# First q of an attention and soft-MoE kernel: loaded in f32 on SyncE's queue and cast by ScalarE

## The chip, the cores and the metric

The kernel runs on one core of a Trainium2 chip. The metric is the device time of one execution in microseconds (us), and a smaller number is better. Five engines work side by side, each with its own list of instructions, in order: TensorE (PE), VectorE (DVE), ScalarE (ACT), GpSimd (POOL) and SyncE (SP). POOL and SP also issue transfers between HBM and the on-chip memory (SBUF); all of these are carried by the same 16 DMA engines. In the profile the queue `q0 software_dynamic` holds what POOL issues and `q1 hardware_dynamic` what SP issues. A load issued by POOL may convert its data on the way (f32 in HBM, bf16 in SBUF); a load issued by SP copies them as they are.

## The reference

Attention with a causal mask over 4 batches and 8 heads of 768 rows of 64, where five of the heads see only the first 4 positions and a window of 64; its output, as 3072 rows of 512, goes through a soft mixture of 8 experts with 4 slots each.

```python
scores = scale * np.matmul(q, k.transpose(0, 1, 3, 2))           # (4, 8, 768, 768)
stream_keep = causal & (is_sink | in_win)
mask = np.where(retr, full_mask, stream_mask)                    # by head
a = softmax(np.where(mask, scores, -1e9))
x = (a @ v).transpose(0, 2, 1, 3).reshape(3072, 512)

logits = x @ phi                                                 # (3072, 32)
d = softmax(logits, axis=0); c = softmax(logits, axis=1)
slot_input = (d.T @ x).reshape(8, 4, 512)
for e in range(8):
    slot_out[e] = np.maximum(slot_input[e] @ w1[e], 0) @ w2[e]   # w1 512x1024, w2 1024x512
out = c @ slot_out.reshape(32, 512)
```

All inputs are f32 in HBM: q, k and v 6.3 MB each, w1 and w2 16.8 MB each. The output is 6.3 MB.

## The kernel before

**Staging.** q, k and v of a batch are loaded as 96 partitions by 2 x 2048 values, converted to bf16 on the way, into one of 12 buffers of 8 KB per partition (`slots`). TensorE transposes them (`Tq`, `Tk`, `Tv`; four pieces of 16 transposes, line 421) into one of two PSUM buffers of class `TR`, and DVE or ACT copies them out (`Eq`, `Ek`, `Ev`; lines 237 and 239). For each of 16 pairs of heads the scores come in five groups: a matmul `QK` (line 451), an exponential on ACT `EX` (line 518) into `pt`, a mask product on DVE `MK` (line 463), and the product with v `PV` (line 566). Per batch the logits, their exponential and the slot sums follow. Behind the last batch come the two expert layers (`H`, line 734; `W2`, line 793) and the output rows (`OM`, `OE`, line 818 and on), stored by SP.

**Order.** The order of all work is written out by hand in the string `ORDER`: each word is one step, and the steps are emitted in that sequence, so each engine gets its instructions in it. A letter behind a slash picks the engine of a copy. `Z..` and `warm` are matmuls on zeros that fill TensorE's idle time.

**Loads.** POOL issues all loads of q, k, v, w1 and w2 (`Lq0` is q of batch 0, `Lw3` the fourth expert's w1, `Lw15h1` the second half of the last w2). They are numbered round eight semaphores, so a load waits until the one eight before it has landed. Most also wait for a free buffer. SP issues three small loads at the start: `Lri`, the heads' flags (8 KB spread to 128 partitions), and `Lphi0` and `Lphi1`, the two halves of phi (32 KB each in pieces of 128 bytes), and at the end the stores.

**The start.** The steps that matter here are these. `tables` (POOL, lines 299 to 301) writes index rows. `ident` and `keypos` (DVE) turn them into the identity matrix and distances. `flags` (DVE, line 321 and on) needs `Lri`; behind it stand `hm0` and `hm3` (masks of four heads, lines 331 and 332), `slotbits` (lines 335 to 338), and then the copies `Eq0.0` and `Eq0.1`. On POOL `slottab` (lines 341 to 345) waits for `slotbits`. `phi` (ACT, line 383) needs both phi loads and stands ahead of the first exponential, `EX.0.1`. On PE the step `warm` runs first, then `Tq0.3` and `Tq0.2` (copied out by ACT), the filler `Z0`, then `Tq0.0` and `Tq0.1` (copied out by DVE), then k of batch 0.

Of the kernel before, what the change touches and what calls it, by code (L numbers as in the profile page):

```python
# [25 lines left out]
QK.1.1 PV.0.3 PV.0.4 QK.1.3 Lk1.32 VF.1/D MK.1.2 EX.1.1 PV.0.5 Lv1.0 QK.2.3 VB.2/D Lv1.64 Tq1.0 NM.0 MK.1.1
EX.1.3 QK.2.4 Tq1.1 PV.1.0 EX.2.3 MK.1.3 PV.1.1 Ek1.0.0/D EX.2.4 QK.1.4 PV.1.2 PV.1.3 QK.2.1 Eq1.0/D Ek1.1.0/D
Eq1.1/D Tq1.2 EX.1.4 QK.2.0 MK.1.4 Tk1.2 Eq1.2/D EX.2.1 Lw1 Ek1.2.0/D PV.1.4 Lw2 VF.2/P Ek1.2.32/D MK.2.3
EX.2.0 Ev1.2.0/A PV.1.5 NM.1 MK.2.0 QK.2.2 Z67 EX.2.2 Tk1.1 Lq2 Ev1.1.0/D Lk2 QK.3.0 Ek1.1.32/D Tk1.0 PV.2.0
VF.3/P QK.3.1 EX.3.0 Ev1.0.0/D Tk1.3 QK.3.2 EX.3.1 Ek1.0.32/D MK.2.2 MK.2.1 Tq1.3 MK.2.4 QK.3.3 Lv2.0 PV.2.1  # L30
PV.2.2 PV.2.3 MK.3.0 EX.3.2 MK.3.1 Lv2.32 QK.3.4 Lq3.0 PV.2.4 PV.2.5 Ev1.3.0/D Ek1.3.0/D EX.3.3 Eq1.3/D EX.3.4
Z65 MK.3.2 NM.2 QK.4.2 QK.4.1 V2.5 PV.3.0 Ek1.3.32/A PV.3.1 MK.3.3 MK.3.4 EX.4.2 V2.4 PV.3.2 QK.4.3 PV.3.3
VB.4/D PV.3.4 PV.3.5 EX.4.1 Lq3.64 QK.4.0 MK.4.2 VB.5/D EX.4.3 XT.2 EX.4.0 NM.3 XT.0 VF.4/P Z66 XE.0/D QK.5.0
MK.4.0 MK.4.1 XE.2/A QK.5.2 EX.5.0 PV.4.0 XT.3 XT.1 PV.4.1 EX.5.2 PV.4.2 XE.3/D QK.4.4 XE.1/D MK.4.3 Tv1.0
Eq2.0/D LG.0 EX.4.4 Tv1.1 Ev1.0.64/D Tv1.3 MK.5.2 EL.0 Ev1.1.64/A MK.5.0 Eq2.1/D QK.5.1 PV.4.3 TE.0 Eq2.3/D
Lw3 QX.1 Ev1.3.64/D EX.5.1 MK.4.4 EXX.1 Tv1.2 EG.0/D DS.0 QK.5.3 VF.5/P MK.5.1 PV.4.4 PV.4.5 Eq2.2/D
Ev1.2.64/A QK.6.2 SA.0 V2.6 EX.5.3 QK.5.4 NM.4 V2.7 VB.6/D PV.5.0 EX.6.2 EX.5.4 Lw4 PV.5.1 QK.6.1 Tk2.0 MK.6.2
EX.6.1 PV.5.2 Lw5 VB.7/D MK.5.3 QK.6.0 Ev2.0.0/D Tk2.1 PV.5.3 QK.6.3 MK.5.4 Ek2.0/D MK.6.1 Lk3 EX.6.0 PV.5.4
EX.6.3 Ek2.1/D Ev2.1.0/D VF.6/P PV.5.5 QK.7.1 Tk2.3 MK.6.0 EX.7.1 QK.6.4 Tk2.2 NM.5 QK.7.0 MK.6.3 Ek2.3/D
Ev2.3.0/D EX.6.4 MK.6.4 PV.6.0 MK.7.1 PV.6.1 Ev2.2.0/D PV.6.2 PV.6.3 QK.7.2 XT.5 PV.6.4 PV.6.5 EX.7.0 XE.5/D  # L40
QK.7.4 MK.7.0 VF.7/P EX.7.2 XT.4 Ek2.2/A NM.6 EX.7.4 XE.4/D QK.7.3 EX.7.3 V2.8 PV.7.0 PV.7.1 MK.7.2 QK.8.0
Tv2.0 PV.7.2 MK.7.4 QK.8.1 VB.8/D Ev2.0.32/D Eq3.0.0/D Tv2.2 EX.8.0 QK.8.2 XT.6 MK.7.3 Ev2.2.32/D EX.8.1
PV.7.3 MK.8.0 XE.6/D Eq3.2.0/D QK.8.3 EX.8.2 EX.8.3 PV.7.4 Lv3 PV.7.5 MK.8.1 NM.7 Tv2.1 QK.9.0 Tv2.3 Eq3.1.0/A
Lw6 VF.8/P QX.2 EX.9.0 Ev2.1.32/D Lw7 Ev2.3.32/D PV.8.0 XT.7 Eq3.3.0/D Lw8 EXX.2 PV.8.1 XE.7/D MK.8.2 QK.8.4
V2.9 VB.9/D V2.11 PV.8.2 EX.8.4 VB.11/A LG.1 MK.8.4 VF.9/P MK.8.3 QK.9.1 PV.8.3 EL.1 V2.10 PV.8.4 VF.11/D
MK.9.0 VB.10/D EX.9.1 QK.9.3 TE.1 PV.8.5 EG.1/D EX.9.3 MK.9.1 QK.9.2 DS.1 QK.9.4 NM.8 Tq3.0 SA.1 EX.9.2 PV.9.0
EX.9.4 PV.9.1 Eq3.0.64/D QK.10.1 XT.8 QK.10.2 Ek3.0/D MK.9.2 XE.8/D Tq3.1 PV.9.2 EX.10.1 MK.9.3 QK.10.0 MK.9.4
Lw9 Ek3.1/D Tq3.2 EX.10.2 PV.9.3 Eq3.2.64/D Ek3.2/D QK.10.3 VF.10/P PV.9.4 PV.9.5 Eq3.1.64/D EX.10.0 MK.10.2
QK.11.0 Tq3.3 EX.10.3 QK.10.4 NM.9 MK.10.0 EX.11.0 Tv3.0 QK.11.2 PV.10.0 MK.10.1 Ev3.0/D PV.10.1 MK.10.3
PV.10.2 EX.10.4 QK.11.1 MK.11.0 MK.10.4 EX.11.2 XT.9 PV.10.3 EX.11.1 Eq3.3.64/D QK.11.4 Lw10 Ek3.3/D PV.10.4  # L50
EX.11.4 XE.9/D PV.10.5 QK.12.1 Tv3.3 EX.12.1 NM.10 QK.11.3 Tv3.2 QK.12.0 EX.11.3 Ev3.3/D PV.11.0 MK.11.1 Tv3.1
EX.12.0 QX.3 Ev3.2/D MK.11.2 XT.10 Ev3.1/D PV.11.1 QK.12.2 EXX.3 MK.11.3 MK.12.0 V2.12 EX.12.2 MK.11.4 VB.12/D
PV.11.2 QK.12.4 MK.12.1 PV.11.3 PV.11.4 EX.12.4 Lw11 XE.10/D QK.12.3 VF.12/P EX.12.3 PV.11.5 QK.13.1 Lw12
NM.11 MK.12.3 V2.13 MK.12.2 QK.13.0 MK.12.4 XT.11 XE.11/D EX.13.1 PV.12.0 PV.12.1 EX.13.0 QK.13.2 PV.12.2
PV.12.3 QK.13.4 EX.13.2 MK.13.0 EX.13.4 PV.12.4 PV.12.5 QK.13.3 LG.2 MK.13.2 NM.12 VB.13/A VF.13/D MK.13.1
EX.13.3 V2.14 QK.14.1 VB.14/D PV.13.0 V2.15 EL.2 EX.14.1 PV.13.1 MK.13.3 QK.14.0 PV.13.2 QK.14.2 VB.15/D
MK.13.4 MK.14.1 Lw13 PV.13.3 EX.14.0 EX.14.2 PV.13.4 VF.14/P VF.15/P QK.14.3 PV.13.5 MK.14.0 QK.14.4 EX.14.3
TE.2 NM.13 EX.14.4 XT.12 EG.2/D QK.15.0 PV.14.0 MK.14.3 PV.14.1 MK.14.2 MK.14.4 XT.13 XE.13/D QK.15.1 PV.14.2
EX.15.0 EX.15.1 PV.14.3 QK.15.2 XE.12/D PV.14.4 PV.14.5 EX.15.2 QK.15.3 EX.15.3 MK.15.1 QK.15.4 MK.15.0 NM.14
MK.15.2 DS.2 PV.15.0 EX.15.4 MK.15.3 PV.15.1 MK.15.4 XT.14 PV.15.2 PV.15.3 Lw14 XE.14/A SA.2 PV.15.4 PV.15.5  # L60
LTa LGa.3 NM.15 XT.15 XE.15/D Z1 LTb ET LGb.3 Z2 EL.3 DS.3 SA.3 RC Z3 SI Z4 SIE EE.3/D H.0.1 H.0.0 EE.0/D
H.1.0 HR.0.1/D HR.0.0/A TH.0 H.1.1 EE.1/D HE.0/D W2.0 W2.1 HR.1.0/A HR.1.1/A Lw15h0 TH.1 HE.1/D W2.2 W2.3 W2.4
EE.2/D W2.5 W2.6 Lw15h1 W2.7.0 SO.0/A RWa RWRa OMf0L OMf1L OEf1L/D RWb OMf2L RWRb OMf3L OMf4L OEf2L/D OEf0L/A
OEf3L/A OMf5L W2.7.1 OEf4L/A OMf6L SO.1/A OMf7L STl0.0 OMf0R OMf1R OMf2R OEf6L/A OEf5L/D OEf1R/A STl0.2 OMf3R
OEf7L/D OEf0R/D OMf4R OMf5R OMf6R STl1.0 OMf7R OMf8 OEf3R/A OMf9 OEf6R/A OEf2R/D OEf4R/D OMf10 OMf11 STl1.2
# [79 lines left out]
def kernel(  # L145
# [95 lines left out]
    def load(name, eng, nbytes, buf, dst, src, deps=()):  # L241
        e = {"POOL": nc.gpsimd, "SP": nc.sync}[eng]
        return pl.op(name, eng, deps=deps, acq=[buf] if buf else [], info=("dma", nbytes),
                     emit=lambda o: e.dma_start(dst(), src))  # L244
# [656 lines left out]
```

## Time and profile before

| | |
|---|---|
| median of 3 runs | 149.55 us (149.5 to 149.68) |
| the profiled execution | 149.39 us, of which the span from first to last instruction is 147.6 us |
| PE busy | 128.8 us (87% of the span) |
| DVE busy | 115.9 us (78%) |
| ACT busy | 104.9 us (71%) |
| POOL busy | 36.4 us (25%) |
| DMA | 32.89 MB written at a mean of 223 GB/s; HBM read 52.5 MB |
| granted TensorE clock, mean | 0.964 |

Busy shares are averages over stages with different limits. The DMA line of the page counts written bytes: a converting load writes half of what it reads. Times in the timeline count from the span's start; a row gives the start, the duration, the engine, the line and the tiles, and in brackets how long the engine stood idle before and what released it. A row of the transfers gives the median time from issue to landing.

### The profile page before, as it was taken

The page shows a single profiled execution, that of the slowest core. Times are in us where ns is not written, and L with a number is a line of the kernel's source. Part 1 is how long each engine was busy: PE and PEld are TensorE (multiplying, and loading weights), DVE is VectorE, ACT ScalarE, POOL GpSimd, SP SyncE. Part 2 cuts the span into 40 slices and gives each one's busy share as a digit, 9 for nine tenths or more (in the row PEclk, how much of TensorE's full clock was granted, in tenths as well). Part 3 has the DMA queues.
Part 4 walks back from the last instruction along what each step waited for, and adds up shares of the span by engine and source line. Part 5 has one row for each costly group of instructions (what it writes and reads, how often), then busy time and mean ns, then how long its engine had stood idle before and what let it go on. Part 6 is the DMA issues. An engine that isn't in the chain of part 4 may idle for free.

```text
span 147.6 us, 5037 instructions
## 1 busy us (share of the span) xinstructions
PE 128.8 (87%) x2196; PEld 82.2 (56%) x2204; DVE 115.9 (78%) x273; ACT 104.9 (71%) x129; POOL 36.4 (25%) x59
## 2 busy tenths in 40 slices
...
DMA  3999999999999999999999999999999999889995
GB/s 31 197 217 220 216 208 213 212 222 215 212 212 214 214 216 223 220 215 209 206 218 220 213 215 215 218 218 218 215 215 218 218 206 190 119 276 361 422 413 233
DMA packets 10373, 32.89 MB, mean 223 GB/s; under 512 B 1392, under 2 KB 5488, under 8 KB 8048
## 3 DMA queue, kind: packets, MB, share of 16 engines
...
HBM read 52.50 MB, written 6.29 MB: 398 GB/s over the span
## 4 chain that ended last, share of the span: by engine, by line
PE 34%; DMA 24%; DVE 18%; ACT 8%; POOL 4%; issue 4%; ACTq 0%; POOLq 0%; DVEq 0%
DMA slot<-in_v_dram 12%; DMA qk<-in_moe_w_dram 12%; PE ps L566 9%; PE ps L451 8%; PE ps L421 7%; DVE pt L463 6%; ACT pt L518 4%; DVE xv L579 4%; ACT slot L824 3%; PE ps L818 2%; POOL slot L244 2%; PE ps L591 2%; PE ps L605 2%; DVE vx L239 1%; DVE qk L239 1%
## 5 line engine op out<-in xcount | busy, mean ns | idle before, releaser
L518 ACT ACTIVATE pt<-ps 128x1024 bf16<-128x1024 f32 x80 | 77.4, 1035 | 8.0 <-PE ps L451 7.2
L463 DVE TENSOR_TENSOR pt<-pt,msk 128x512 bf16<-128x512 bf16 (+1 forms) x80 | 38.2, 505 | 0.7 <-ACT pt L518 0.7
L451 PE MATMUL ps<-qk 64*128 64x512 bf16 (+3 forms) x256 | 32.5, 309 | 0.2
L566 PEld LDWEIGHTS <-pt 128*128 128x128 bf16 x640 | 25.1, 97 | 9.4 <-issue 6.2
L566 PE MATMUL ps<-vx,pt 128*128 128x65 bf16 x352 | 28.5, 193 | 1.0 <-DVE pt L463 0.4
L421 PE MATMUL ps<-ident,slot 128*64 128x128 bf16 (+1 forms) x640 | 22.8, 216 | 2.6 <-DMA slot<-in_q_dram 1.1
L498 POOL TENSOR_TENSOR vf<-vx,fm 128x528 bf16<-128x528 bf16 x12 | 13.9, 1164 | 44.5 <-DVE vx L239 42.1
L421 PEld LDWEIGHTS <-slot 128*64 128x64 bf16 (+1 forms) x640 | 17.7, 109 | 10.7 <-issue 8.7
L566 PE MATMUL ps<-vf,pt 128*128 128x65 bf16 x288 | 22.8, 195 | 0.0
L239 DVE COPY qk<-ps 128x768 bf16<-128x768 bf16 (+2 forms) x35 | 15.3, 466 | 6.0 <-PE ps L421 4.8
L359 PE MATMUL ps<-zero 128*128 128x512 bf16 x51 | 15.2, 412 | 1.8 <-DVE zero L350 1.2
L579 DVE TENSOR_TENSOR xv<-ps,rs 128x768 bf16<-128x768 f32 x16 | 15.3, 957 | 0.6
L451 PEld LDWEIGHTS <-qk 64*128 64x128 bf16 x256 | 9.3, 94 | 8.2 <-issue 2.7
L239 DVE COPY xT<-ps 128x768 bf16<-128x768 bf16 (+1 forms) x16 | 8.9, 569 | 3.2 <-PE ps L755 2.3
L244 POOL DMA_DIRECT2D slot<-in_moe_w_dram x12 | 7.1, 589 | 14.5 <-PE ps L421 12.0
L824 ACT ACTIVATE slot<-ps,rrow 128x512 f32<-128x512 f32 (+1 forms) x17 | 8.8, 588 | 2.2 <-PE ps L818 2.2
L826 DVE TENSOR_SCALAR slot<-ps,rrow 128x256 f32<-128x256 f32 (+1 forms) x15 | 8.5, 603 | 1.8 <-PE ps L818 1.1
L818 PE MATMUL ps<-msk,xv 128*128 128x256 bf16 (+1 forms) x31 | 8.0, 381 | 1.7 <-ACT slot L824 0.9
L239 DVE COPY xv<-ps 128x768 bf16<-128x768 bf16 (+2 forms) x21 | 8.9, 430 | 0.7 <-PE ps L421 0.4
L359 PEld LDWEIGHTS <-zero 128*128 128x128 bf16 x58 | 5.3, 103 | 7.5 <-issue 2.7
L237 ACT COPY qk<-ps 128x768 bf16<-128x768 bf16 (+1 forms) x5 | 3.5, 713 | 7.0 <-PE ps L421 7.0
L239 DVE COPY vx<-ps 128x768 bf16<-128x768 bf16 x14 | 7.7, 553 | 0.6 <-PE ps L482 0.6
...
## 6 DMA issues: line engine op xcount, KB each, us to landing
...
```

What stands on the lines that cost most here:

```text
L239: nc.vector.tensor_copy(dst, src)
L244: emit=lambda o: e.dma_start(dst(), src))
L359: nc.tensor.matmul(scb[buf.slot][:, 0, :], zero[:, 0:128], zero, start=True, stop=True)
L421: nc.tensor.transpose(t[64 * i:64 * (i + 1), :, s, :], rv[:, i, 8 * c + s, :], ident[0:rows, 0:rows])
L451: nc.tensor.matmul(scb[sc.slot][:, i, c:c + 128 * nb], kk, qq.rearrange("p b c -> p (b c)"), start=True, stop=True)
L463: e.tensor_tensor(pT[:, :, 0:w], pT[:, :, 0:w], mh[:, :, c:c + w], op=ALU.mult)
L498: e.tensor_tensor(vfs[VFb[p].slot], vv, mm, op=ALU.mult)
L518: nc.scalar.activation(pTs[PTb[b, n].slot][:, :, 512 * g:512 * (g + 1)], scb[sc.slot], ACT.Exp, scale=scale)
L566: nc.tensor.matmul(pvb[:, h, 65 * i:65 * (i + 1)], lt, rhs, start=(j == 0), stop=(j == i))
L579: nc.vector.tensor_tensor(xo, pvw[:, :, :, 0:64], r.rearrange("p i (j o) -> p i j o", o=1).to_broadcast([P, 2, 6, 64]), op=ALU.mult)
L818: nc.tensor.matmul(bank()[:, b0:b0 + c1 - c0], out_lhs(gi, r), slot_out[:, c0:c1], start=True, stop=True)
L824: nc.scalar.activation(d, s_, ACT.Copy, scale=sc_)
```

## The change

`Lq0`, one converting load on POOL, becomes four plain loads on SP. Each brings 512 of the 2048 values per row half (96 x 2 pieces of 2 KB), in the order 3, 2, 0, 1, into the memory of `pt` read as f32. ACT casts each part into the same buffer as before (`Cq0.3`, `Cq0.2`, `Cq0.0`, `Cq0.1`). A transpose `Tq0.c` now needs only its own part, where before it needed the whole load. On SP the four loads stand ahead of `Lri`, `Lphi0` and `Lphi1`. On POOL `tables` comes first, and the loads from `Lw0` to `Lw2` (with `ones` among them) stand ahead of `slottab`, where they stood behind it. The order of the loads among themselves is as before.

```diff
-zero Lri warm Lq0 tables ident keypos Tq0.3 Tq0.2 Eq0.3/A Eq0.2/A Z0 Tq0.0 flags hm0 Lk0 hm3 Tq0.1 Lv0
-slotbits slottab Eq0.0/D Eq0.1/D Z62 Tk0.2 Tk0.1 Ek0.2/D Ek0.1/D Lphi0 Z64 Lphi1 Tk0.3 Tk0.0 Z61 Lw0 Ek0.3/D
+zero Lq0.3 Lq0.2 Lq0.0 Lq0.1 Lri Lphi0 Lphi1 warm tables ident keypos Cq0.3 Cq0.2 Cq0.0 Cq0.1 Tq0.3 Tq0.2
+Eq0.3/A Eq0.2/A Z0 Tq0.0 flags hm0 Lk0 hm3 Tq0.1 Lv0 Lw0 ones Lq1 Lk1.0 Lk1.32 Lv1.0 Lv1.64 Lw1 Lw2 slotbits
+slottab Eq0.0/D Eq0.1/D Z62 Tk0.2 Tk0.1 Ek0.2/D Ek0.1/D Z64 Tk0.3 Tk0.0 Z61 Ek0.3/D Ek0.0/D phi Z63 QK.0.1
...
+    q32 = pt_mem[0:96, 0:16 * KB].bitcast(F32).rearrange("p (i x) -> p i x", i=2)
+
+    def load_q0():
+        src = srcs["q"][0].rearrange("(i n) (t s) d -> n t i (s d)", i=2, s=32).rearrange("n t i x -> (n t) i x")
+        for c in (3, 2, 0, 1):
+            cc = slice(512 * c, 512 * (c + 1))
+            a = load(f"Lq0.{c}", "SP", 96 * 2 * 2048, None, lambda cc=cc: q32[:, :, cc], src[:, :, cc])
+            lands[0, c] = pl.op(f"Cq0.{c}", "ACT", deps=[a], acq=[tbufs[0]], emit=lambda o, cc=cc: nc.scalar.copy(
+                slots[tbufs[0].slot][0:96, :].rearrange("p (i x) -> p i x", i=2)[:, :, cc], q32[:, :, cc]))
...
-    load_qkv("q", 0)
+    load_q0()
...
-            a = pl.op(f"T{x0}{b0}.{c}", "PE", deps=[lands[g, p[0], p[1]] for p in parts] + [o_id] + wait,
+            a = pl.op(f"T{x0}{b0}.{c}", "PE", deps=([lands[g, p[0], p[1]] for p in parts] if g else [lands[0, c]]) + [o_id] + wait,
```

SP's list from its start, before. The first load is `Lri`, the next two are phi; the rest are stores of the output.

```order
L244 DMA eT<-in_is_retrieval_dram 128x16
L244 DMA eT<-in_moe_phi_dram 64x4x32 x2
L862 DMA out_dram<-slot_66 128x2x256 [waits DMASW3_49,DVE_49,Activation_49]
L862 DMA out_dram<-slot_66 128x2x256 [waits DVE_49,Activation_49]
L862 DMA out_dram<-slot_70 128x2x256 [waits DMASW1_49,DVE_49,Activation_49]
```

And of the changed kernel:

```order
L244 DMA pt<-in_q_dram 96x2x512 x4
L244 DMA eT<-in_is_retrieval_dram 128x16
L244 DMA eT<-in_moe_phi_dram 64x4x32 x2
L874 DMA out_dram<-slot_66 128x2x256 [waits DMASW2_49,DVE_49,Activation_49]
L874 DMA out_dram<-slot_66 128x2x256 [waits DMAHW0_49,DVE_49,Activation_49]
```

The four parts of q stand ahead of the flags and of phi, in one queue.

POOL's list behind its preamble, before: q, the index rows, k and v of batch 0, then the slot tables (lines 341 to 345), and behind them the first w1.

```order
L244 DMA slot_63<-in_q_dram 96x2x2048
L299 IOTA xT 128x128
L300 IOTA pc_i 128x1
L301 IOTA xT 128x256
L244 DMA slot_64<-in_k_dram 96x2x2048
L244 DMA slot_65<-in_v_dram 96x2x2048
L341 TENSOR_SCALAR sum_96<-xT,pc 128x32 [waits DVE_49,Pool_49]
L342 TENSOR_TENSOR pc<-pc 128x1
...
L345 MEMSET cols 128x1
L244 DMA slot_66<-in_moe_w_dram 128x4096
```

And of the changed kernel:

```order
L311 IOTA xT 128x128
L312 IOTA pc_i 128x1
L313 IOTA xT 128x256
L244 DMA slot_64<-in_k_dram 96x2x2048
L244 DMA slot_65<-in_v_dram 96x2x2048
L244 DMA slot_66<-in_moe_w_dram 128x4096
...
L244 DMA slot_70<-in_moe_w_dram 128x4096 [waits DMASW0_49]
L244 DMA slot_71<-in_moe_w_dram 128x4096 [waits DMASW1_49]
L353 TENSOR_SCALAR sum_96<-xT,pc 128x32 [waits DVE_49,Pool_49]
```

The load of q has gone from the head of the list, the index rows come first, and ten loads now precede the slot tables; the last two of these wait for the landing of k and v of batch 0.

ACT's list from its start, before: the copies of `Tq0.3` and `Tq0.2`, the cast of phi, the exponentials.

```order
L237 ACT_TABLE_LOAD
L237 COPY qk_75<-ps 128x24x32 [waits PE_49] x2
L383 CAST phi_89<-eT 128x512 [waits DMAHW2_49,DMAHW1_49]
L518 ACTIVATE pt<-ps 128x2x512 [waits PE_49] x7
L534 ACTIVATE vx_78<-ps 128x1024 [waits PE_49]
```

And of the changed kernel:

```order
L271 ACT_TABLE_LOAD
L271 CAST slot_63<-pt 96x2x512 [waits DMAHW0_49]
L271 CAST slot_63<-pt 96x2x512 [waits DMAHW1_49]
L271 CAST slot_63<-pt 96x2x512 [waits DMAHW2_49]
L271 CAST slot_63<-pt 96x2x512 [waits DMAHW3_49]
L237 COPY qk_75<-ps 128x24x32 [waits PE_49] x2
L395 CAST phi_89<-eT 128x512 [waits DMAHW6_49,DMAHW5_49]
L530 ACTIVATE pt<-ps 128x2x512 [waits PE_49,Activation_49]
```

Four casts, each waiting for one part, stand ahead of the two copies. DVE's list is the same in both kernels.

More of the change, by code (lines that the diff above doesn't have):

```diff
@@ L26 @@
[L26 to L65, printed above, removed]
@@ new lines @@
+Tv0.0 QK.0.0 EX.0.1 hm2 hm1 EX.0.0 Tv0.1 Ev0.0/D QK.0.2 Ev0.1/D EX.0.2 Tv0.3 QK.1.0 EX.1.0 Ev0.3/D Tv0.2
+QK.0.4 MK.0.1 Ev0.2/D V2.0 EX.0.4 V2.3 QK.0.3 MK.0.0 Z60 QK.1.2 VB.0/D VB.3/D MK.0.2 EX.0.3 V2.1 MK.1.0 VF.0/D
+MK.0.4 QX.0 MK.0.3 EX.1.2 VB.1/D PV.0.0 V2.2 EXX.0 PV.0.1 PV.0.2 QK.1.1 PV.0.3 PV.0.4 QK.1.3 VF.1/D MK.1.2
+EX.1.1 PV.0.5 QK.2.3 VB.2/D Tq1.0 NM.0 MK.1.1 EX.1.3 QK.2.4 Tq1.1 PV.1.0 EX.2.3 MK.1.3 PV.1.1 Ek1.0.0/D EX.2.4
+QK.1.4 PV.1.2 PV.1.3 QK.2.1 Eq1.0/D Ek1.1.0/D Eq1.1/D Tq1.2 EX.1.4 QK.2.0 MK.1.4 Tk1.2 Eq1.2/D EX.2.1
```

46 lines of the change are left out of this document (40 added, 6 removed).

## The prediction

> **What bounds the kernel now.** I read the page's slices first, then the stages of the transfers, then the chain of waits, then PE's own waits.
>
> ```profile
> span 147.6 us, 5037 instructions
> ...
> DMA  3999999999999999999999999999999999889995
> GB/s 31 197 217 220 216 208 213 212 222 215 212 212 214 214 216 223 220 215 209 206 218 220 213 215 215 218 218 218 215 215 218 218 206 190 119 276 361 422 413 233
> ```
>
> The DMA engines are full from the second slice on. While inputs stream they write about 215 GB/s of bf16, which is 430 GB/s of f32 read; plain stores at the end move 422 GB/s. So q in f32 should take the engines as long as q converted on the way (1.57 MB at 430 GB/s, 3.7 us): no term for the format. What is lost is at the start:
>
> ```profile
> 2.00:3.00 1.00, 1.00 (x4) 0.43 (x3) 0.38 (x3) 0.02 (x1) 0.91 (x4) 1.00 0.47 49
> 3.00:4.00 1.00, 1.00 (x4) 0.33 (x3) 0.79 (x6) 0.00 (x0) 1.00 (x3) 1.00 0.93 106
> 4.00:5.00 1.00, 1.00 (x6) 0.46 (x5) 0.93 (x3) 0.00 (x0) 0.43 (x1) 1.00 0.93 180
> 5.00:12.00 7.00, 5.79 (x101) 3.55 (x101) 4.15 (x24) 1.50 (x2) 2.78 (x10) 1.00 1.10 216
> 12.00:119.00 107.00, 102.92 (x1847) 67.82 (x1855) 96.52 (x219) 90.36 (x104) 30.38 (x40) 1.00 1.04 215
> ```
>
> The last column is GB/s, ahead of it the share of the DMA engines. The full rate is there from 5 us on, and then until 119. Three rows of the chain of waits, with its two long DMA pieces:
>
> ```profile
> 12.88 18.41 DMA slot<-in_v_dram
> ...
> 44.37 0.47 DVE xT L239
> ...
> 112.01 17.10 DMA qk<-in_moe_w_dram
> ```
>
> The last is the last expert weight, issued at 112 and landed at 129.1 behind the stream. It looks like a kernel bound by its transfers, which an earlier stream would shorten. But PE hardly waits for them:
>
> ```profile
> 12.32 0.74 PEld L421 LDWEIGHTS <-slot 96*64 96x64 bf16 x32 [0.42 <-DMA slot<-in_k_dram]
> ...
> 16.43 0.40 PEld L421 LDWEIGHTS <-slot 96*64 96x64 bf16 x16 [0.25 <-DMA slot<-in_v_dram]
> ...
> 26.75 0.64 PE L421 MATMUL ps<-ident,slot 128*64 128x128 bf16 x16 [0.69 <-DMA slot<-in_k_dram]
> ...
> 31.43 0.64 PE L421 MATMUL ps<-ident,slot 128*64 128x128 bf16 x16 [0.78 <-DMA slot<-in_v_dram]
> ...
> 126.54 0.40 PE L793 MATMUL ps<-qk,xT 128*32 128x256 bf16 x8 [0.51 <-DMA qk<-in_moe_w_dram]
> ...
> 129.15 0.40 PE L793 MATMUL ps<-qk,xT 128*32 128x256 bf16 x8 [0.24 <-DMA qk<-in_moe_w_dram]
> ```
>
> The last four brackets, waits of PE for a load, add up to 2.2 us; the first two, of its weight loads at the start, to 0.7. Between 31 and 126 us no row of PE waits for a load, and the three compute engines are each busy for 84 to 96% of the stage (102.92, 96.52 and 90.36 of 107 us). So stream and compute run side by side, nearly level: **both must start earlier to gain, and one that starts more than some 2 us later costs what exceeds it.**
>
> **The change, part by part.** The start of each engine:
>
> ```profile
> 0.74 0.38 SPq L244 DMA_DIRECT2D eT<-in_is_retrieval_dram  x1
> 1.17 1.41 SPq L244 DMA_DIRECT2D eT<-in_moe_phi_dram  x2
> ...
> 1.30 0.80 POOL L244 DMA_DIRECT2D slot<-in_q_dram  x1 [0.85 <-POOLq L882]
> ...
> 2.19 0.27 POOL L299 IOTA xT<- 128x128 f32 x1
> ...
> 2.47 0.71 POOL L301 IOTA xT<- 128x256 f32 x1
> ...
> 6.44 0.64 PE L364 MATMUL ps<-zero 128*128 128x1 bf16 x20
> ...
> 8.13 0.87 PE L421 MATMUL ps<-ident,slot 96*64 96x96 bf16 x32 [1.05 <-DMA slot<-in_q_dram]
> ...
> 8.70 1.50 ACT L237 COPY qk<-ps 128x768 bf16<-128x768 bf16 x2 [6.69 <-PE ps L421]
> ...
> 12.00 0.62 ACT L383 CAST phi<-eT 128x512 bf16<-128x512 f32 x1 [1.80 <-DMA eT<-in_moe_phi_dram]
> ...
> 16.51 1.02 ACT L518 ACTIVATE pt<-ps 128x1024 bf16<-128x1024 f32 x1 [3.89 <-PE ps L451]
> ```
>
> *The stream.* The flags' first bytes and q's first bytes:
>
> ```profile
> GB/s 6 8 8 6 9 6 6 6 8 8 8 6 6 8 6 6 8 6 8 6 26 57 98 102 398 243 53 60 139 142 126 136 313 12 112 3 3 102 12 118
> ...
> GB/s 7 7 7 7 7 6 7 7 9 60 104 351 55 106 143 249 14 58 60 73 67 55 55 164 109 164 218 109 164 109 109 218 218 328 109 164 109 328 218 109
> ```
>
> The first row covers 1.8 to 3.5 us, the second 2 to 5. SP's flags, issued at 0.74, move from 1.8 on, 1.1 later; POOL's q, issued at 1.30, from about 2.8, 1.5 later. With q at the head of SP's queue the stream begins at 1.8 instead of 2.8: gain up to **1.0 us**, if compute follows. PE could: its warm-up ends at 7.1 (6.44 + 0.64) and `Tq0.3` started at 8.13.
>
> *q against k.* POOL's index rows took 2.19 to 3.18 (2.47 + 0.71), so with them at 1.30 k is issued at 2.3 and moves from 3.8. Until then SP's queue has 2.0 us alone. POOL's own ramp wrote 0.33 MB in 2.3 us where 0.5 is the full rate, 0.8 us lost; with the same ramp SP moves 1.2 us x 430 GB/s = 0.53 MB, 258 of q's 768 pieces of 2 KB. About **510 are left when k arrives**, with the flags and phi behind them. How the two queues share is the question, and the trace has one case of it: phi's second half, behind the first POOL load.
>
> ```profile
> eT<-in_is_retrieval_dram SPq DMA_DIRECT2D x1, 8.0 KB, 2.7
> ...
> eT<-in_moe_phi_dram SPq DMA_DIRECT2D x2, 32.0 KB, 6.3
> ...
> eT<-in_moe_phi_dram SPq DMA_DIRECT2D x1, 32.0 KB, 10.0
> ...
> DMA packets 117, 0.48 MB, mean 184 GB/s; under 512 B 0, under 2 KB 0, under 8 KB 117
> ...
> q0 software_dynamic: 155, 0.63, 104.3%
> q1 hardware_dynamic: 77, 0.01, 4.1%
> ```
>
> Of the two phi loads the second took 10.0 us and the first 2.6 (the median of both is 6.3), for 32 KB. From 3.6 to 6.2 (the row of 117 packets) none of SP's small packets moved at all. From 8 to 11 (the last two rows) SP's queue got 77 packets while POOL's got 155. So a queue gets packets, not bytes: POOL's 8 KB reads against SP's small ones, at best one to one.
>
> One to one, a POOL packet lasts 16 x 3/155 = 0.31 us on its engine, one of q's 2 KB at 27 GB/s per engine 0.08: 16/0.39 = 41 pieces per us. 510 pieces then take 12.4 us and q ends at 16. The other bound is that SP's queue keeps the engines to itself until q is through (2.4 us at full rate): 6.3. I take **12.5**, nearer the first, since the row is of this very case, but with some credit for the pieces already in the engines and for the gaps between POOL's loads. The flags, 128 packets at 52 per us (155/3), follow at **15** (bounds 9 and 18). Phi's 512 packets take another 10 us at that rate: **22 to 25** (bounds 18 and 28).
>
> *What is queued behind the flags.*
>
> ```profile
> 5.29 0.17 DVE L321 TENSOR_SCALAR xT<-eT 128x16 f32<-128x16 int32 x1
> ...
> 8.66 0.17 DVE L338 CAST pc<-pc_i 128x3 f32<-128x3 int32 x1
> ...
> 11.41 1.02 DVE L239 COPY qk<-ps 128x768 bf16<-128x768 bf16 x2 [2.58 <-PE ps L421]
> ```
>
> On DVE `flags`, four masks and `slotbits` fill 5.29 to 8.83, and only behind them stand the copies of `Tq0.0` and `Tq0.1`, at 11.41. Flags at 15 put these at 15 + 3.5 = 18.5, which is **7 us late**, and with them the two transpose buffers, k's transposes and the first scores. On ACT four casts of 1024 values (1.0 each by the row of 16.51) precede the copies of `Tq0.3` and `Tq0.2`: q whole at 12.5 gives 12.5 + 1.0 + 0.75 + 0.6 for the next transpose, 15, which is covered by DVE's 18.5. Phi precedes `EX.0.1` on ACT: 23 + 0.6 against 16.5 is 7 again, level with the scores, so it adds nothing.
>
> *POOL.* Ten loads ahead of `slottab`: the last waits for v of batch 0, as it did before, and from 5 us on the engines were full without them, so no byte arrives earlier for it. `slottab` itself, then issued at some 17 us, is needed by the first `XE`, the copy into `xT` at 44 in the chain above. Nothing, and cover of 25 us. The lanes' waits shift with the load taken out and pair the same loads.
>
> *The sum.* Compute 7.0 later; PE's waits for loads fall away, 2.2 us on PE and some 0.3 of the weight loads', minus **2.5** of the 2.9 that all six brackets hold. From 149.39 us of the profiled execution: 149.39 + 7.0 - 2.5 = 153.9, and with the 0.16 by which the median stands above it, **154.0 us**. With flags at 11.5 it is 150.6, with 18 it is 157.
>
> The Trainium skill, "DMA: Bandwidth & Descriptors", section "Queues, rings and completion order", says that an engine changes between queues only after a packet of some 9 to 17 descriptors. The row from 3.6 to 6.2 agrees, the rows from 8 to 11 (small packets all along) do not.
>
> **The rivals.**
>
> *SP's queue goes first* and empties before k takes over. For: it has a 2 us lead, and POOL's own first load held phi off for that long. Against: in 8 to 11 neither queue went first. Then flags are there by 7, DVE's copies by 10.5, all moves by the stream's gain: 149.55 - 1.0 = 148.5, bounds 148.0 and 149.2.
>
> *The delay is eaten.* Flags at 9 to 10, phi by 19: compute 1.5 to 2.7 late, PE's waits of 2.5 absorb it: 149.3 to 149.8.
>
> *A whole POOL load goes ahead each time a part of q is through* (k from 3.8, v, w0, each 3.7 to 4.8 us at 215 GB/s, 1.6 us for two parts between). Flags at 17.6, DVE's copies at 21, 9.7 late; phi behind the next load, at 22 or more: 149.55 + 9.7 - 2.5 = 156.8, to 161 if phi waits another two loads. The skill's rule named above would make this one.
>
> *No change in the start*, if ACT and DVE did not depend on the late loads: the lists exclude it, since each engine takes its instructions in order.
>
> **How the numbers follow.** Forecast 154.0 with its own range, 150.6 to 157: 0.60. SP first: 0.22. Eaten: 0.08, of which 0.06 within 0.2%. Whole loads: 0.10. A measurement of this kernel tells 0.2%, 0.3 us, from no change. Faster 0.24, same 0.06, slower 0.70. The range leaves out part of the whole loads above and of SP first below: 148.5 to 157.5.
>
> **What would show it.** The first PE row of q near 7.1 (right in either case). Landing of the flags' load: over 10 us from issue for the forecast, under 5 for SP first. DVE idle some 8 to 10 us ahead of line 333 with the flags' load as releaser. The ACT row of the phi cast behind 20 us. POOL's first k issue near 2.3. PE's brackets at 26 and 31 gone. The forecast is wrong if the flags land before 9 us, or if compute makes up for the delay between 30 and 110 us, where I count no slack.

## The result, and the profile after

The changed kernel takes 161.58 us (median of 6 runs, 159.68 to 162.62) against 149.53 us for the kernel before beside it: a ratio of **1.076, 95% interval [1.070, 1.082]**. Slower, as forecast (154.0), but 7.6 us beyond it and 4 us outside the range. Runs over 1.5% above the fastest of their kernel (here two of the six) are left out of the ratios and of the differences between kernels below, and where that moves a median, the one without them stands in brackets (here 161.18). The profiled execution took 161.32 us, its span 159.5.

The page's slices of the changed kernel (one digit or number per 4 us):

```profile
span 159.5 us, 5057 instructions
...
PEclk9997559879999999999999999999999999999855
DMA  3999999999999999999999999999993899169994
GB/s 113 273 226 228 211 214 211 220 215 222 185 215 212 215 140 210 220 218 208 214 221 222 212 216 218 199 164 205 218 210 78 138 183 196 22 207 354 415 415 189
```

The transfer engines are full from the second slice on, and faster there than before (273 GB/s written in the second slice against 197). PE's granted clock, 1.0 throughout that stretch before, falls to a half in the fifth and sixth slice (16 to 24 us) and dips again in the eighth and ninth (28 to 36 us). The start, from the timeline (start, duration, engine, line, operation; in brackets how long the engine was idle before it, and what ended that):

```profile
0.71 1.86 SPq L244 DMA_DIRECT2D pt<-in_q_dram  x4
1.74 0.81 POOL L244 DMA_DIRECT2D slot<-in_k_dram  x1
2.62 0.46 SPq L244 DMA_DIRECT2D eT<-in_is_retrieval_dram  x1
3.12 1.62 SPq L244 DMA_DIRECT2D eT<-in_moe_phi_dram  x2
8.41 0.87 PE L433 MATMUL ps<-ident,slot 96*64 96x96 bf16 x32
13.63 1.04 ACT L271 CAST slot<-pt 96x1024 bf16<-96x1024 f32 x1 [4.18 <-DMA pt<-in_q_dram]
15.42 1.55 PE L433 MATMUL ps<-ident,slot 96*64 96x96 bf16 x32 [4.31 <-ACT qk L237]
16.29 0.17 DVE L333 TENSOR_SCALAR xT<-eT 128x16 f32<-128x16 int32 x1 [12.08 <-DMA eT<-in_is_retrieval_dram]
19.86 1.02 DVE L239 COPY qk<-ps 128x768 bf16<-128x768 bf16 x2
25.75 0.39 PE L463 MATMUL ps<-qk 64*128 64x512 bf16 x2
27.77 0.62 ACT L395 CAST phi<-eT 128x512 bf16<-128x512 f32 x1 [11.71 <-DMA eT<-in_moe_phi_dram]
28.30 4.70 ACT L530 ACTIVATE pt<-ps 128x1024 bf16<-128x1024 f32 x5
34.09 2.15 ACT L530 ACTIVATE pt<-ps 128x1024 bf16<-128x1024 f32 x2 [1.09 <-PE ps L463]
47.25 4.90 ACT L530 ACTIVATE pt<-ps 128x1024 bf16<-128x1024 f32 x5 [0.62 <-PE ps L463]
```

The last part of q is there at 13.6 (forecast 12.5), the flags at 16.3 (15), DVE's copies start at 19.86 (18.5). The scores' first matmul is done at 26.1, but the first exponential starts at 28.30, behind the cast of phi, which came at 27.7 (forecast 22 to 25). Before, the first exponential was at 16.51: **11.8 us late**, where the forecast had 7. One later row of before shows what of it is made up:

```profile
34.86 4.90 ACT L518 ACTIVATE pt<-ps 128x1024 bf16<-128x1024 f32 x5 [0.62 <-PE ps L451]
```

The same group stands at 47.25 after, 12.4 late, and the span ends 11.9 late. Nothing is made up. The chain of waits of the changed kernel names the one piece that covers the start:

```profile
3.90 23.79 DMA eT<-in_moe_phi_dram
```

The transfers, from 2 to 5 us (one line) and from 8 to 11 (two):

```profile
q1 hardware_dynamic: 384, 0.74, 79.8%
...
q0 software_dynamic: 112, 0.46, 75.2%
q1 hardware_dynamic: 113, 0.23, 31.7%
```

Until 5 us SP's queue (q1) is alone: k, issued at 1.74, has not moved a packet. From 8 to 11 the queues take turns, 112 packets to 113, as the prediction had it. But q alone moved 0.74 MB in 3 us, 245 GB/s, not 430, with the engines busy for 80% of that time.

### The profile page after: what moved, and what is told of

Its sections match the earlier page's. It is cut to its first block, busy times and chain, and to the rows that moved or that the text cites. A ratio compares the mean times of both kernels' runs of the same rounds, so it can differ in the third digit from the quotient of the medians.

```text
span 159.5 us, 5057 instructions
## 1 busy us (share of the span) xinstructions
PE 133.7 (84%) x2204; PEld 84.7 (53%) x2204; DVE 116.7 (73%) x273; ACT 108.8 (68%) x133; POOL 35.5 (22%) x58
## 4 chain that ended last, share of the span: by engine, by line
PE 46%; DVE 19%; DMA 15%; ACT 8%; issue 3%; SPq 2%; ACTq 0%
DMA eT<-in_moe_phi_dram 15%; PE ps L578 10%; PE ps L463 9%; DVE pt L475 9%; PE ps L433 7%; DVE xv L591 4%; ACT pt L530 4%; ACT slot L836 3%; PE ps L617 3%; PE ps L494 3%; PE ps L371 2%; PE ps L746 2%; PE ps L805 2%; PE ps L603 2%; SPq L244 2%
## 5 line engine op out<-in xcount | busy, mean ns | idle before, releaser
L475 DVE TENSOR_TENSOR pt<-pt,msk 128x512 bf16<-128x512 bf16 (+1 forms) x80 | 38.8, 513 | 0.8 <-ACT pt L530 0.8
L463 PE MATMUL ps<-qk 64*128 64x512 bf16 (+3 forms) x256 | 33.0, 313 | 2.2 <-ACT pt L530 2.0
L578 PEld LDWEIGHTS <-pt 128*128 128x128 bf16 x640 | 25.2, 97 | 10.4 <-issue 6.2
L433 PE MATMUL ps<-ident,slot 128*64 128x128 bf16 (+1 forms) x640 | 24.7, 227 | 6.5 <-ACT qk L237 4.3
L433 PEld LDWEIGHTS <-slot 128*64 128x64 bf16 (+1 forms) x640 | 19.6, 117 | 15.2 <-issue 14.9
L371 PE MATMUL ps<-zero 128*128 128x512 bf16 x58 | 18.8, 464 | 1.2 <-DVE zero L362 1.2
L271 ACT CAST slot<-pt 96x1024 bf16<-96x1024 f32 x4 | 4.2, 1045 | 8.5 <-DMA pt<-in_q_dram 8.5
L333 DVE TENSOR_SCALAR xT<-eT 128x16 f32<-128x16 int32 x1 | 0.2, 175 | 12.1 <-DMA eT<-in_is_retrieval_dram 12.1
L395 ACT CAST phi<-eT 128x512 bf16<-128x512 f32 x1 | 0.6, 617 | 11.7 <-DMA eT<-in_moe_phi_dram 11.7
```

The source lines that it names most:

```text
L371: nc.tensor.matmul(scb[buf.slot][:, 0, :], zero[:, 0:128], zero, start=True, stop=True)
L433: nc.tensor.transpose(t[64 * i:64 * (i + 1), :, s, :], rv[:, i, 8 * c + s, :], ident[0:rows, 0:rows])
L463: nc.tensor.matmul(scb[sc.slot][:, i, c:c + 128 * nb], kk, qq.rearrange("p b c -> p (b c)"), start=True, stop=True)
L475: e.tensor_tensor(pT[:, :, 0:w], pT[:, :, 0:w], mh[:, :, c:c + w], op=ALU.mult)
L578: nc.tensor.matmul(pvb[:, h, 65 * i:65 * (i + 1)], lt, rhs, start=(j == 0), stop=(j == i))
```

## The experiments

All times are medians; ratios are against the kernel before, run beside it.

**The POOL half alone.**

```diff
 hm0 Lk0 hm3 Tq0.1 Lv0
-slotbits slottab
+Lw0 ones Lq1 Lk1.0 Lk1.32 Lv1.0 Lv1.64 Lw1 Lw2 slotbits slottab
```

> Only the POOL half of the change: q loaded as before by POOL, the loads from Lw0 to Lw2 issued ahead of the slot tables. Packet theory (the loss is SP's queue sharing the DMA engines packet by packet with POOL's, so that the flags and phi come late): nothing in that is touched, 149.5 us, within 0.3. Rival A (the ten loads on POOL ahead of the slot tables hold POOL, and through it DVE or the later loads): several us of the 12 show up here, 152 to 158.

149.63 us, 1.0013 [0.9989, 1.0037]. By itself this half costs and brings nothing, as the prediction said.

**Small loads ahead of q**, on SP's queue of the changed kernel.

```diff
-zero Lq0.3 Lq0.2 Lq0.0 Lq0.1 Lri Lphi0 Lphi1
+zero Lri Lphi0 Lphi1 Lq0.3 Lq0.2 Lq0.0 Lq0.1
```

> The changed kernel with the flags and phi ahead of q's four parts on SP. Packet theory: the flags land near 3.5 us and phi near 4, as before; the last part of q still shares with k and comes near 14.5, so ACT's copy of the first transposes ends near 16.5 and DVE's copies start near 17 instead of 19.9, the first exponential near 22.3 instead of 28.3; the time falls from 161.3 to some 155.5. Rival B (the small loads do not matter, the late last part of q does it all): no change, 160 to 161.5.

173.71 us, 1.161 [1.157, 1.165]: far from every number expected. q's first and last cast in its timeline, and both queues from 5 to 8 us:

```profile
17.15 1.04 ACT L271 CAST slot<-pt 96x1024 bf16<-96x1024 f32 x1 [15.15 <-DMA pt<-in_q_dram]
...
32.50 1.04 ACT L271 CAST slot<-pt 96x1024 bf16<-96x1024 f32 x1 [3.69 <-DMA pt<-in_q_dram]
```

```profile
q0 software_dynamic: 156, 0.61, 102.5%
q1 hardware_dynamic: 156, 0.02, 8.3%
```

156 packets to 156, with phi's small ones against POOL's larger ones. The sharing is packet for packet; what I had not seen is that q, issued at 2.58 behind k (1.74), also lost its head start. q was in at 32.5 us instead of 13.6.

**phi's cast late**: in the changed kernel the cast moved back on ScalarE to its first use.

```diff
-Ek0.3/D Ek0.0/D phi Z63 QK.0.1
+Ek0.3/D Ek0.0/D Z63 QK.0.1
...
-VB.5/D EX.4.3 XT.2
+VB.5/D EX.4.3 phi XT.2
```

> The changed kernel with the cast of phi moved on ACT from ahead of the first exponential to ahead of the first XT.2 (phi is first used by the logits at some 50 us). Packet theory: phi, landing at 27.5, was what held the first exponential by 2.1 us beyond the scores (25.75 to 28.3), the flags hold the rest: first exponential near 26.3, the time falls by some 2, to 159.3. If phi alone were the cause, it would fall by the 11.7 us that ACT waited, to 150; if the flags alone, no change.

157.31 us (157.18), 1.050 [1.047, 1.053]: 4.0 less than the changed kernel, 2.0 more than I had expected. Its timeline:

```profile
25.68 5.73 ACT L530 ACTIVATE pt<-ps 128x1024 bf16<-128x1024 f32 x6 [9.32 <-PE ps L463]
...
42.89 4.90 ACT L530 ACTIVATE pt<-ps 128x1024 bf16<-128x1024 f32 x5 [0.62 <-PE ps L463]
```

The first exponential is 2.6 us earlier than after the change, and from there to the group quoted above it is 17.2 us, against 18.35 before (16.51 to 34.86) and 18.95 after. So 1.1 us are made up here, which the changed kernel does not get. Seven of the runs below, with their first exponential at quite different times, take 17.2 us for this stretch too.

**A delay of known size.** The kernel before, with 19 more matmuls on zeros (4.05 us of PE) ahead of the first scores.

```diff
-        fill(f"Z6{i}", 3, tq0)
+        fill(f"Z6{i}", 22 if i == 3 else 3, tq0)
```

> The kernel before with 19 more matmuls on zeros in the filler just ahead of the first scores (19 x 0.213 = 4.05 us at the full clock), all loads as before: compute is put back by 4 us while PE stays busy. The prediction's slack (2.5 us of PE's waits for loads fall away): 149.5 + 4.05 - 2.5 = 151.1. No slack (the waits overlap other limits): 153.6. If about 151, the 2.5 us missing in the changed kernel went to PE's lower clock there.

152.18 us, 1.0173 [1.014, 1.0206]: 2.65 us for 4.05 (in the profiled execution the first exponential is 4.2 late). The slack is **1.4 us, not 2.5**.

The next four runs start from the changed kernel with phi's cast late (157.18).

**k held until q is there**: a one-column POOL copy ahead of k's issue that reads q's last part.

```diff
+        pl.op("hold", "POOL", deps=[x for x in pl.ops if x.name == "Lq0.1"],
+              emit=lambda o: nc.gpsimd.tensor_copy(scr[0:96, 0:1], q32[:, 0, 512:513]))
```

> The changed kernel with the phi cast late (157.31 us as measured), and k's first load on POOL held behind a one-column POOL copy that waits for q's last part, so that q has the engines alone. Theory (q is late because its 2 KB packets alternate with POOL's from 6 us on): q's last part lands at 7.5 to 8.5, the flags by 9, the DVE copies of q's transposes near 12; k is issued near 8.5 and lands near 14; time 150.5 to 152. Rival (the four parts, their f32 format and the four casts cost the time by themselves): q's last part still lands behind 11, time 155 or more.

156.04 us (the profiled execution, 154.11, is the shortest of four), 1.040 [1.034, 1.046]: q came in as the theory said, the time did not. The last cast, k's issue and k's first transpose, and the queue from 5 to 8 us:

```profile
9.06 1.04 ACT L272 CAST slot<-pt 96x1024 bf16<-96x1024 f32 x1 [0.17 <-DMA pt<-in_q_dram]
...
9.22 0.82 POOL L245 DMA_DIRECT2D slot<-in_k_dram  x1
...
16.84 1.41 PE L437 MATMUL ps<-ident,slot 96*64 96x96 bf16 x32 [4.01 <-DMA slot<-in_k_dram]
```

```profile
q1 hardware_dynamic: 604, 0.81, 104.9%
```

Alone on the engines, q is in at 9.06 instead of 13.92 (the run it starts from), so sharing cost it 4.9 us. But alone it still moves at 0.81 MB in 3 us, 270 GB/s, with the engines fully busy. That, and k waiting its turn until 16.8 (12.3 before), is why the median falls by only 1.1.

**Flags first**, ahead of q's four parts.

```diff
-zero Lq0.3 Lq0.2 Lq0.0 Lq0.1 Lri
+zero Lri Lq0.3 Lq0.2 Lq0.0 Lq0.1
```

> The changed kernel with the phi cast late (157.31 us), and the flags' 8 KB load moved ahead of the four parts of q on SP's queue. If waiting behind q is what makes the flags late: flags by 4 us, DVE no longer idle for them, and the DVE copies then wait for q itself (q's last part at about 14.5, the copies at 16.6 instead of 19): time near 154.5. If the queue that is first keeps the engines, and SP's second load now comes behind k: q's parts are spread over more than 20 us as in the run with all small loads first, time 165 or more.

160.14 us, 1.070 [1.065, 1.075]; between the two cases, and 3.0 slower than the run it starts from. The flags were there at 4.1 and DVE never waited for them, but q's parts were issued 0.4 us later, only two of them went ahead of k instead of three, and the last one arrived at 18.2 instead of 13.9. q is then the last releaser.

**q as one load in 8 KB pieces**, with the same four casts behind it.

```diff
-            a = load(f"Lq0.{c}", "SP", 96 * 2 * 2048, None, lambda cc=cc: q32[:, :, cc], src[:, :, cc])
+        a = load("Lq0", "SP", 96 * 2 * 8192, None, lambda: q32, src)
```

> The changed kernel with the phi cast late (157.31 us), q as one f32 load of SP in 8 KB pieces (192 packets instead of 768), with the same four casts behind it. Theory (queues share by packets, not by bytes): against POOL's 8 KB packets q now gets four times the bytes per packet; q whole at 9 to 10, flags at 12.5, first scores 3 to 4 us earlier: time near 153.5. Rival (sharing by bytes, or the f32 format alone): q's end stays at 13 to 14, and since no cast can start before the whole load is in, the time is 157.5 to 159.

154.50 us, 1.0327 [1.0309, 1.0344], 2.7 less, in the direction of the packet theory (153.5). The same bytes in a quarter of the packets:

```profile
10.43 3.89 ACT L271 CAST slot<-pt 96x1024 bf16<-96x1024 f32 x4 [8.42 <-DMA pt<-in_q_dram]
...
12.90 0.18 DVE L333 TENSOR_SCALAR xT<-eT 128x16 f32<-128x16 int32 x1 [8.69 <-DMA eT<-in_is_retrieval_dram]
```

q is whole at 10.4. k's first packets came at 7.7, although issued at 1.75. The flags, issued at 1.17 and so ahead of k as well, did not go ahead of it: they landed at 12.9.

**Flags first and k held** until the third part of q is there, phi's cast late.

```diff
-zero Lq0.3 Lq0.2 Lq0.0 Lq0.1 Lri
+zero Lri Lq0.3 Lq0.2 Lq0.0 Lq0.1
...
-flags hm0 Lk0
+flags hm0 hold Lk0
```

> All remedies together: flags ahead of q's parts on SP's queue, phi's cast late, k's first load on POOL held until the third of q's four parts (columns 1024 to 1535) has landed. Theory: q's last part at about 8.5 to 9, flags by 4, DVE copies near 11, k landed by 13.5, as before the change or 1 us later: time 149.5 to 151. Faster than before only if the 1 us that q starts earlier reaches the end: 148.5. Rival (the casts and f32 parts cost by themselves): 153 or more.

152.66 us (152.33), 1.0189 [1.0157, 1.0222]. The first exponential is at 18.96, 2.45 late, and the time 2.7: with these remedies for the order together, q in f32 still costs 1.9%.

**k issued later** (phi's cast late, as in the run after it): two spare index rows on POOL, so that k is issued at 2.97, behind all of q and the flags, but waits for nothing.

```diff
+        for i in range(2):
+            nc.gpsimd.iota(scr[:, i], [[1, 64], [64, 4]], base=0, channel_multiplier=0, ...)
```

> The changed kernel with the phi cast late (157.31 us), and two spare index rows of 0.7 us each on POOL ahead of k's issue, so that k is issued at about 3.1 instead of 1.74, behind the issue of all four parts of q (0.71 to 2.57) and of the flags (2.62). If what SP has issued ahead of k's issue goes ahead of k: q's last part at 8 to 9, flags by 9.5, k right behind without the gap that holding it for q's landing left; time 152 to 153.5. If k comes in by the clock, some 4.4 us after its issue whatever was issued ahead of it, so at 7.5, and then alternates: q's last part at 11, flags at 12.5, time 154.5 to 155.5. If it always comes in at 6: unchanged, 157.3.

152.81 us over eight runs, four at 151.0 to 151.6 and four at 154.0 to 155.0; the bracketed median (151.25), the ratio of 1.010 [1.007, 1.014] and the profile are of the first four. No trace of the other four was kept, so what they lose is open. From the timeline and the queues from 7.5 to 8.5 us, in two halves:

```profile
9.55 1.04 ACT L272 CAST slot<-pt 96x1024 bf16<-96x1024 f32 x1 [0.50 <-DMA pt<-in_q_dram]
9.86 0.17 DVE L336 TENSOR_SCALAR xT<-eT 128x16 f32<-128x16 int32 x1 [5.33 <-DMA eT<-in_is_retrieval_dram]
```

```profile
q1 hardware_dynamic: 69, 0.11, 103.4%
q0 software_dynamic: 1, 0.00, 4.0%
...
q1 hardware_dynamic: 131, 0.08, 77.1%
q0 software_dynamic: 12, 0.05, 48.4%
```

k's first packet moves at about 8, when q is nearly through, and in the next half microsecond SP's queue, with most of the flags, still moves 131 packets to k's 12. **A delay of k's issue by 1.2 us brings 5.9 us** (157.18 to 151.25) in the first four runs. The edit adds work and removes none, so what it bought is the order.

**PE kept busy**: 19 and 14 more matmuls on zeros where PE waits for q and its copies (phi's cast late).

```diff
-fill("Z0", 8, tlast)
+fill("Z0", 27, tlast)
-        fill(f"Z6{i}", 3, tq0)
+        fill(f"Z6{i}", 17 if i == 2 else 3, tq0)
```

> The changed kernel with the phi cast late (157.31 us), with 19 and 14 more matmuls on zeros where PE waits for q and for the copies of its transposes (9 to 15.5 and 16.4 to 20 us); nothing else depends on them. If PE's idle time is what halves its granted clock from 13 to 23 us, the clock stays at 1.0 there, k's transposes take 0.9 us instead of 1.5, the first exponential comes 1.0 to 1.4 us earlier and the time is near 156.1. If the clock is not in it, or the stretch is covered by other waits: 157.3, and slower if the added matmuls run into the waiting ones.

157.63 us (156.40), 1.045 [1.039, 1.051]: 0.8 less than 157.18, but the two intervals overlap, so that by the time alone no difference can be told. The stretches show what changed. The columns are the window, its length, busy time of PE, its weight loads, DVE, ACT and POOL, the granted clock, the transfer engines' share and GB/s. First the changed kernel, then this one:

```profile
12.00:17.00 5.00, 1.58 (x33) 1.45 (x33) 0.64 (x5) 2.44 (x3) 0.57 (x1) 0.66 1.13 222
17.00:20.00 3.00, 1.36 (x3) 0.30 (x3) 2.83 (x16) 0.00 (x0) 0.54 (x1) 0.50 1.04 214
20.00:24.00 4.00, 3.54 (x57) 2.30 (x58) 1.99 (x4) 0.00 (x0) 1.08 (x5) 0.51 1.09 212
...
31.00:34.00 3.00, 2.89 (x31) 1.69 (x28) 2.05 (x5) 2.00 (x3) 0.00 (x0) 0.50 1.09 225
```

```profile
12.00:17.00 5.00, 4.42 (x49) 2.30 (x48) 0.37 (x3) 2.44 (x3) 0.57 (x1) 1.00 1.15 225
17.00:20.00 3.00, 3.00 (x15) 1.35 (x15) 2.79 (x17) 0.00 (x0) 0.54 (x1) 1.00 1.01 205
```

With PE busy the clock stays at 1.0, so its idling halves it. DVE's first copy with phi's cast late alone, and below it the same copy and the first exponential of this run:

```profile
19.34 1.02 DVE L239 COPY qk<-ps 128x768 bf16<-128x768 bf16 x2
```

```profile
20.06 1.02 DVE L239 COPY qk<-ps 128x768 bf16<-128x768 bf16 x2
25.05 5.73 ACT L530 ACTIVATE pt<-ps 128x1024 bf16<-128x1024 f32 x6 [8.65 <-PE ps L463]
```

From the copy to the first exponential it took 5.0 us (20.06 to 25.05) here, 6.3 (19.34 to 25.68) with phi's cast late alone: the half clock's price is **1.3 us**, read from one profile of each. In this profile DVE's copy starts 0.7 us later, which hides half of it.

**Half of q, and a quarter, by SP**, with phi's cast late; POOL brings the rest, converting, as its first load (the diff is that for the half; for the quarter `Lq0.2` goes to POOL too).

```diff
-zero Lq0.3 Lq0.2 Lq0.0 Lq0.1 Lri Lphi0 Lphi1 warm tables
+zero Lri Lq0.3 Lq0.2 Lphi0 Lphi1 warm Lq0 tables
```

> A version meant to beat both: flags first on SP's queue, then q's columns 1024 to 2047 in f32 by SP with two casts, while POOL brings columns 0 to 1023 converting on the way, as its first load, and then k; phi last on SP with its cast late. If the converting load is the faster one (430 GB/s of f32 against some 260 of a plain load) and SP only fills the 1 us ahead of POOL's first bytes: q whole at 7 to 7.5, k 0.5 to 1 us earlier than before the change, time 148.5 to 149.3. If the plain halves slow POOL's one down: q whole at 8.5 to 9, time 150 to 151.

> As the run with halves, but SP brings only one quarter of q in f32 (columns 1536 to 2047) and POOL the other three, converting. SP's quarter, 0.39 MB, fits nearly into the time from 1.8 to 2.8 us in which POOL's first load does not move yet. If that time is what there is to gain: q whole at 7, k 0.7 us earlier than before, time 148.7 to 149.3, and not worse than with halves. If the order of the start does not matter any more: 149.5.

150.15 us, 1.0034 [1.0013, 1.0056], and 150.22, 1.0039 [1.0016, 1.0063]: neither beats the kernel before. The quarter got its earlier start, and in its profiled execution (150.93, 0.7 above the median) gave it back at the next batch's v:

```profile
16.10 7.07 ACT L536 ACTIVATE pt<-ps 128x1024 bf16<-128x1024 f32 x7 [6.64 <-PE ps L469]
...
31.92 0.98 PE L439 MATMUL ps<-ident,slot 128*64 128x128 bf16 x16 [1.84 <-DMA slot<-in_v_dram]
```

The first exponential is 0.4 us earlier than before, and PE then waits 1.84 us for a load, 0.78 before. v's transposes start 0.5 us later than before (31.43), and PE's granted clock is 0.50 from 32.1 to 35.4. That the extra bytes of f32 are what puts v back is a reading and was not tried by itself.

**The q half alone**: POOL's later loads put back behind the slot tables, in the changed kernel.

```diff
-Lv0 Lw0 ones Lq1 Lk1.0 Lk1.32 Lv1.0 Lv1.64 Lw1 Lw2 slotbits slottab
+Lv0 slotbits slottab
...
-Z61 Ek0.3/D Ek0.0/D phi
+Z61 Lw0 Ek0.3/D Ek0.0/D ones phi
```

> The other half of the change alone: the changed kernel (161.58 us) with POOL's later loads put back behind the slot tables, where they stood before. The loads ahead of the tables cost and brought nothing in the kernel before (149.63 against 149.53). If they are without effect here too: 161.6. If they matter here, since the tables' operation on POOL waits for the flags by way of VectorE and so now stands until 20 us: the first expert weight is issued at about 20.5 instead of 3.2, the engines run dry from about 19 to 22, the second batch's loads come 3 us later than in the changed kernel, and the time is 162.5 to 164.5.

158.21 us, 1.058 [1.053, 1.063]. Neither case: **the half that costs nothing alone costs 3.0 us inside the change** (161.18 against 158.21), and I had expected it to help. The phi cast, the first exponential, and the stretch from 17 to 20 us:

```profile
17.42 0.62 ACT L395 CAST phi<-eT 128x512 bf16<-128x512 f32 x1 [0.70 <-DMA eT<-in_moe_phi_dram]
...
27.14 5.74 ACT L530 ACTIVATE pt<-ps 128x1024 bf16<-128x1024 f32 x6 [9.10 <-PE ps L463]
```

```profile
17.00:20.00 3.00, 2.02 (x19) 0.84 (x15) 2.83 (x17) 0.62 (x1) 0.00 (x0) 0.50 0.02 5
```

POOL's queue runs out ahead of 17 us, and phi, with nothing to take turns with, is in at 17.4 instead of 27.7. The engines then stand idle (0.02 of their time) until the first expert weight is issued at 21.25, and no cost of that can be seen: this run is 1.0 us above the one with phi's cast late, and its first exponential 1.5 us later.

**q in f32 by POOL's queue**: the kernel before, q's first load whole in f32, four casts behind it.

```diff
+        a = load("Lq0", "POOL", 96 * 2 * 8192, None, lambda: q32, src)
```

> The kernel before with one thing changed: q's first load is still POOL's first, whole and in 8 KB pieces, but brought in f32 without conversion, with the four ScalarE casts behind it. If the format is what makes q slow (a plain f32 load writes 240 to 280 GB/s, a converting one reads 430): q is there at 9.2 to 9.8 instead of 7.9, k at 13.5 to 14, the first exponential 2 to 3 us later with the casts, time 150.5 to 152. If it is SP's queue or its small pieces that are slow and POOL's queue brings f32 at 430 GB/s: q at 7.9 as before, only the casts (1.0 us each, two on the path) in between, k at 12.3 as before: 149.5 to 150.2.

154.20 us, 1.032 [1.024, 1.040], beyond even the format's case. The casts, and both queues from 5 to 8 us:

```profile
11.03 3.88 ACT L271 CAST slot<-pt 96x1024 bf16<-96x1024 f32 x4 [9.01 <-DMA pt<-in_q_dram]
14.82 1.48 ACT L237 COPY qk<-ps 128x768 bf16<-128x768 bf16 x2
```

```profile
q0 software_dynamic: 82, 0.67, 97.3%
q1 hardware_dynamic: 4, 0.00, 0.2%
```

Alone on the engines, in 8 KB pieces, by the queue that brings converted loads at 430 GB/s of f32: 224 GB/s. So the rate is the format's doing, not that of SP's queue or of the small pieces (the memory that f32 lands in, `pt`, is the same in all these runs and was not varied). q is in at 11.0 instead of 8.1 (issued at 1.30, 6.8 to landing). The rest is the casts: all four, not two, stand ahead of ACT's copies, which start 6.1 us late (14.82 against 8.70), 2.9 of it from the landing and 3.2 from the casts. PE's granted clock is 0.50 from 10.2 to 17 here as well.

## Why the prediction was wrong

The direction, the mechanism and the order of events were right: q shares with k packet by packet, the flags wait behind q, DVE's copies behind the flags, and no gain of the earlier stream reaches the end. The sizes were not, and two of them by more than 2 us. The sum was 7.4 us short in the profiled execution (11.9 instead of 4.5). Four of its steps account for that:

| step, as the prediction put it | forecast | measured | us |
|---|---|---|---|
| DVE's copies | 18.5 | 19.86 | 1.4 |
| copies to first exponential, without phi | 5.1 as before (11.41 to 16.51) | 6.4 (to 26.2, 0.5 behind the scores' 25.75) | 1.3 |
| "level with the scores, so it adds nothing" (phi) | 0 | 2.1 (26.2 to 28.30) | 2.1 |
| "minus 2.5 of the 2.9 that all six brackets hold" | 2.5 | -0.1 (11.8 late at the exponential, 11.9 at the end) | 2.6 |

The last two rows, 4.7 us, hang together: with phi's cast late alone the profiled execution is 4.3 us shorter (161.32 to 157.00). **By size the step that failed most is that phi's wait "adds nothing"**; the earliest one is the next.

*"No term for the format."* This step failed first. I took written bf16 at 215 GB/s as 430 of f32 read, saw stores at 422, and concluded that q in f32 takes 3.7 us. A plain f32 load wrote 224 GB/s (q by POOL) and 270 (k held) with the engines 97% busy or more. At these rates q, 1.57 MB, needs 5.8 to 7.0 us, by either queue. The row that I had, 215 GB/s written, fitted a limit on the bytes written to SBUF as well as one on the bytes read; the runs fit the first far better, though not one single rate.

*q against k.* "258 of q's 768 pieces" by the time that k comes in: 384 packets had moved between 2 and 5 us, and k came in at 6.1, with some 500 of q's pieces gone. The head start was longer than the 2.0 us I gave it, the rate lower. That 12.5 was only 1.1 off is partly luck: one to one from 3.8 on would have given 16 by my own sum, and I picked a number between that and 6.3. One to one from 6.1 on held: 113 of SP's pieces in 3 us, 38 per us where I had 41.

*phi.* It was forecast with the flags' rate, 512 packets in 10 us behind 15, and landed 11.5 us behind the flags; 22 to 25 became 27.7. The forecast's own upper bound was 28, but I called it level with the scores and gave its lateness no price. With the cast late the kernel is 4.0 us shorter; with POOL's later loads put back phi lands at 17.4, no longer holds the first exponential, and the kernel is 3.0 shorter.

*The slack.* Brackets of waits are not all slack: the run with a known delay returns 1.4. The changed kernel returns none. In the one stretch that differs, PE is at half clock again (31 to 34, quoted above), behind the wait for phi. Both runs in which phi holds nothing up (its cast late, and POOL's later loads put back) take 17.2 us from the first exponential to the group quoted above, against 18.95, so the loss goes with that wait; that the second drop of the clock is the link was not tried by itself.

*The half clock.* It was in no term. PE's 4.31 us of waiting ahead of 15.42 is followed by a clock of 0.50 until about 24. The Trainium skill, "TensorE: Matmul & The Clock Gate", Part 1, says that the clock falls to half after an idle window of some 3.4 us; this trace agrees as far as that the fall comes inside the wait of 4.31 us, at 13.6, but it falls a second time, at 30.7, behind a wait of only 1.98. The run with PE kept busy shows the remedy for the first.

*POOL's loads, "nothing".* Right for the kernel before, wrong inside this change: 3.0 us. I asked only whether a byte arrives earlier for them; what mattered is that a queue that never runs out keeps taking every second packet from phi.

The rivals. "SP's queue goes first" was half of the truth (k stood still until 6.1) and is what the run with k issued later makes whole; even then the time is 151.25 in the four shorter runs, not 148.5: q's last part is there at 9.55, where the rival had it through at 6.3. "A whole POOL load goes ahead" gave the nearest time (156.8 to 161) by a mechanism that the trace refutes: 112 packets to 113, with 8 KB reads against 2 KB. The rule of the Trainium skill named in the prediction ("DMA: Bandwidth & Descriptors", "Queues, rings and completion order": 9 to 17 descriptors to a turn) does not show in the windows with both queues busy; the counts there are level, 112 to 113 and 156 to 156, and in the second run they are so half a microsecond at a time (26 to 26 in each half from 6 to 7.5), where turns of nine or more on 16 engines would be expected to scatter. Not level is the row of the kernel before that the prediction rests on, 155 to 77, and why is open.

Of the signals named: the flags' landing over 10 us from issue, phi behind 20 us and the missing brackets at 26 and 31 came as described; the wait ahead of line 333 was 12.1 us, not 8 to 10, and k was issued at 1.74, not 2.3. The first PE row of q was at 8.41, not 7.1, since the warm-up's matmuls ended 1.4 us later (8.0 instead of 6.6); why they did is open.
